# Start sequence, reciprocal rows by head pair, and key sums of pair 4 by adds, in an attention and bilinear feed-forward kernel

## The chip, the cores and the metric

The kernel runs on one core of one Trainium2 chip. Times are device microseconds of one execution; the time of a kernel is the median of its runs. The engines are named as in the profile: PE is TensorE's matmul, PEld its weight load, DVE is VectorE, ACT is ScalarE, POOL is GpSimd and SP is SyncE, which here issues most transfers. ACTq and SPq in a profile are what ScalarE and SyncE issue to their transfer queues.

## The reference

Batch 8, 12 heads, 448 tokens, head dimension 64, all in float32. Attention with normalised queries and keys is followed by a feed-forward block with two factors that are multiplied.

```
def rmsnorm(x, g):
    rms = np.sqrt(np.mean(x * x, axis=-1, keepdims=True) + 1e-06)
    return x / rms * g
q_n, k_n = (rmsnorm(q, g_q), rmsnorm(k, g_k))
scores = 1.0 / np.sqrt(q.shape[-1]) * np.matmul(q_n, k_n.transpose(0, 1, 3, 2))
scores = scores - np.max(scores, axis=-1, keepdims=True)
attn = np.exp(scores)
attn = attn / (np.sum(attn, axis=-1, keepdims=True) + 1e-09)
attn_out = np.matmul(attn, v)                  # (8, 12, 448, 64)
x = attn_out.transpose(0, 2, 1, 3).reshape(3584, 768)
out = (x @ w_a) * (x @ w_b) @ w_out            # w_a, w_b: 768 x 1536; w_out: 1536 x 768
```

## The kernel before, in words

**Attention.** The work is cut into 24 steps called pairs (`p`, three for each of the 8 batches). One step takes four heads as two head pairs `w`, each with two heads `e`. Queries and keys are loaded with half of the heads on partitions 0 to 63 and half on 64 to 127 (`loads`). For every step ScalarE squares q and k (L461, and L473 for the first q), DVE adds the squares up (L463, L485) and scales them (L496, L487), GpSimd raises them to the power -1/2 (L498, L489), and DVE multiplies q by the result (L502, L479 for the first step). TensorE transposes k and q (L537; L561 for the first step, whose q is taken in two parts), and ScalarE copies the transposes to `qkT`, q with the gains (L542, L544, L566, L568).

A step then has seven blocks `j` of keys. `scores` (L585) makes the scores of a block with keys on the partitions, in four products on four quarters of the array, and ScalarE's exponential (L591) turns them into `ET` with the keys' factor as its scale. `values` (L607) adds the block times v into `o`. A group of four products in quarters appears in the trace as 8 matmul records, since each float32 matmul is recorded twice there. Transposes are recorded once.

**Sums over the keys.** The denominators come in one of two ways. For steps below `WIDE` (5 here) `sums_over_keys` multiplies every block by ones on TensorE (L643, seven groups of four products). For the steps from `WIDE` on, `add_up` (L621) first adds the seven blocks on DVE and GpSimd in turn (`ADD_UP`: DVE for j = 1, 3, 5, 6, GpSimd for 2 and 4), and a single group of ones-products takes the sum over the partitions.

**Inversion.** `invert` has ScalarE copy the two sums into `rec` (L656). SP moves one row of each head to 56 partitions (`few`, L663), DVE takes the reciprocal of those 112 x 16 numbers (L689), and SP brings them back. For steps below `SPREAD` (6) they go back into two rows of `rec` (L672), and TensorE spreads the rows over the partitions with ones (`spread`, L679); later steps go by a tensor in memory (L668, L685). DVE multiplies the values by the result (L732).

**Feed-forward.** Two batches form a group `beta`. Its products use recombined factors, so that fewer block products are needed. The weights come as raw words (w_a, w_b and w_out; DMA at L358 and L361 from ScalarE's queue), are rounded in steps (ScalarE L247, DVE L248, L249, L251, L253, L254, L256), combined (L371) and written out to be streamed in again. There are 18 such factors; factors 0 to 11 belong to w_a and w_b, 12 to 17 to w_out. `seq` and `GATES` say in which order and after which block of scores each one starts. The long products are L1288, L865, L989 and L1186.

**What sets the order.** `Plan.op` records every operation with its engine, its costs in a planner and what it reads and writes. `Plan.run` issues the operations in an order that is stored in the text `ORDER`: a list of places, one for each operation. So each engine's sequence is fixed when the kernel is built, and an operation waits, with everything behind it on its engine, until what it reads is there. `op("SP", ...)` is a transfer that SyncE issues.

**The start.** SP issues its half of q, two rows of gains, its half of k, then v; ScalarE issues its halves of q and k, then a first half of a w_out factor. ScalarE's function table is loaded with the first square. TensorE meanwhile multiplies the identity by itself (`warm`, L408: `WARM` blocks of four at first, and `TAIL` blocks after each of the first transposes).

A second path, `general`, stands behind a test on the gains and isn't taken with these inputs.

## Time and profile before

| what | value |
|---|---|
| three runs, median (lowest to highest) | 1489.83 us (1488.78 to 1490.21) |
| the profiled execution | 1492.87 us |
| its span, first to last instruction | 1491.1 us |
| PE busy, share of the span | 1469.9 us, 99% |
| DVE / ACT / POOL busy | 985.9 / 438.7 / 333.2 us |
| mean granted clock of TensorE | 0.994 |

The busy table counts the time in which an engine executes; register, branch and semaphore instructions and the issuing of transfers are left out. Ends of matmuls are modelled, so successive starts tell the pace better than the durations. In a line of the timeline the first number is the start, the second the duration of the merged instructions, and the bracket gives the engine's idle time before it and what ended it. The chain follows the work back from the last instruction, at each step to what released it. In windows the first number in a row is the stretch, the second its length; then come each engine's busy time, the granted clock, the share of the transfer engines, and GB/s.

### The profile page before, as it was taken

The page shows a single profiled execution, that of the slowest core. Times are in us where ns is not written, and L with a number is a line of the kernel's source. Part 1 is how long each engine was busy: PE and PEld are TensorE (multiplying, and loading weights), DVE is VectorE, ACT ScalarE, POOL GpSimd, SP SyncE. Part 2 cuts the span into 40 slices and gives each one's busy share as a digit, 9 for nine tenths or more (in the row PEclk, how much of TensorE's full clock was granted, in tenths as well). Part 3 has the DMA queues.
Part 4 walks back from the last instruction along what each step waited for, and adds up shares of the span by engine and source line. Part 5 has one row for each costly group of instructions (what it writes and reads, how often), then busy time and mean ns, then how long its engine had stood idle before and what let it go on. Part 6 is the DMA issues. An engine that isn't in the chain of part 4 may idle for free.

```text
span 1491.1 us, 21095 instructions
## 1 busy us (share of the span) xinstructions
PE 1469.9 (99%) x7918; PEld 964.2 (65%) x7918; DVE 985.9 (66%) x1571; ACT 438.7 (29%) x792; POOL 333.2 (22%) x173
## 2 busy tenths in 40 slices
PE   8999999999999999999999999999999999999998
PEld 5433444555444555555544445799998899999898
DVE  5886679888765333334667776367677666776786
ACT  5776762121454000001157771011111001111100
POOL 3325551022233000111255651011110001111000
PEclk9999999999999999999999999999999999999999
DMA  9796445555363545446556654555565765555464
GB/s 252 226 256 186 110 113 177 179 200 179 113 167 92 155 147 183 136 160 190 162 142 165 143 138 134 172 157 151 166 175 169 250 180 161 153 154 157 165 211 127
DMA packets 188186, 247.99 MB, mean 166 GB/s; under 512 B 61868, under 2 KB 160684, under 8 KB 181420
## 3 DMA queue, kind: packets, MB, share of 16 engines
q1 hardware_dynamic: 158956, 192.61, 45.3%
q10 hardware_dynamic: 29120, 53.94, 10.6%
q8 instruction: 65, 1.06, 0.3%
q14 instruction: 45, 0.37, 0.1%
HBM read 188.35 MB, written 57.93 MB: 165 GB/s over the span
## 4 chain that ended last, share of the span: by engine, by line
PE 89%; DMA 5%; DVE 3%; issue 1%; ACT 1%; SPq 1%; POOL 0%; ACTq 0%; DVEq 0%; POOLq 0%
PE pq L1288 24%; PE dg L865 17%; PE po L989 16%; PE sc L585 7%; PE o L607 7%; PE da L865 6%; PE g L1186 2%; PE a L1186 2%; PE pt L537 2%; PE su L643 2%; DMA k_sb<-in_k_dram 2%; PE b L1186 1%; PE d L1186 1%; PE e L1186 1%; PE inv L679 1%
## 5 line engine op out<-in xcount | busy, mean ns | idle before, releaser
L1288 PE MATMUL pq<-x,st 128*128 128x448 f32 x1008 | 383.0, 540 | 0.9 <-DVE U L1318 0.9
L1288 PEld LDWEIGHTS pq<-x,st 128*128 128x128 f32 x1008 | 190.3, 190 | 187.8 <-issue 176.6
L591 ACT ACTIVATE ET<-sc,ms 128x448 f32<-128x448 f32 x336 | 191.1, 636 | 67.5 <-PE sc L585 49.5
L498 POOL TENSOR_TENSOR ms<-ms,expo 128x14 f32<-128x14 f32 x47 | 149.2, 3175 | 149.2 <-DVE ms L496 148.2
L865 PE MATMUL dg<-dT,st 128*128 128x224 f32 x672 | 167.2, 354 | 0.5 <-DVE dt L905 0.3
L989 PE MATMUL po<-st,hT 128*128 128x384 f32 x492 | 164.2, 488 | 0.4 <-DMA st<-kept_o 0.4
L865 PE MATMUL dg<-x,st 128*128 128x224 f32 x672 | 162.6, 354 | 0.5 <-DVE dF L912 0.5
L585 PE MATMUL sc<-qkT 64*64 64x448 f32 x1344 | 153.0, 545 | 2.0 <-ACT ET L591 1.7
L607 PE MATMUL o<-ET,v_sb 64*64 64x448 f32 x1344 | 148.9, 542 | 0.0
L893 POOL TENSOR_TENSOR hT<-dF 128x448 f32<-128x448 f32 x42 | 50.3, 1210 | 421.3 <-DVE dF L888 408.6
L989 PEld LDWEIGHTS po<-st,hT 128*128 128x128 f32 x492 | 92.3, 190 | 64.4 <-issue 3.8
L865 PEld LDWEIGHTS dg<-dT,st 128*128 128x128 f32 x672 | 126.5, 190 | 2.6 <-DVE dt L905 0.8
L865 PEld LDWEIGHTS dg<-x,st 128*128 128x128 f32 x672 | 126.2, 190 | 2.8 <-DVE dF L912 1.8
L865 PE MATMUL da<-x,st 128*128 128x224 f32 x504 | 117.3, 353 | 0.0
L621 POOL TENSOR_TENSOR sum<-sum,ET 128x896 f32<-128x896 f32 x38 | 86.9, 2286 | 106.2 <-ACT ET L591 51.7
L585 PEld LDWEIGHTS sc<-qkT 64*64 64x64 f32 x1344 | 47.2, 133 | 84.0 <-issue 44.6
L607 PEld LDWEIGHTS o<-ET,v_sb 64*64 64x64 f32 x1344 | 51.3, 134 | 74.3 <-issue 67.1
L878 ACT COPY dt<-da 128x224 f32<-128x224 f32 x84 | 28.9, 346 | 233.9 <-PE da L865 162.5
L865 PEld LDWEIGHTS da<-x,st 128*128 128x128 f32 x504 | 94.9, 190 | 0.5
L888 DVE TENSOR_TENSOR dF<-dF 128x896 f32<-128x896 f32 x84 | 92.5, 1106 | 2.2
L989 PE MATMUL po<-st,fin 128*128 128x384 f32 x252 | 86.6, 491 | 0.0
L621 DVE TENSOR_TENSOR sum<-sum,ET 128x896 f32<-128x896 f32 x57 | 62.8, 1101 | 30.0 <-POOL sum L621 18.8
(150 smaller groups left out, 1684.3 us busy)
## 6 DMA issues: line engine op xcount, KB each, us to landing
st<-kept_o SPq DMA_DIRECT2D x28, 1152.0 KB
st<-kept_s SPq DMA_DIRECT2D x84, 320.0 KB
kept<-st ACTq DMA_DIRECT2D x12, 1344.0 KB
st<-kept SPq DMA_DIRECT2D x12, 1344.0 KB
st<-kept SPq DMA_DIRECT2D x84, 192.0 KB
ti<-kept_t SPq DMA_DIRECT2D x48, 288.0 KB
kept_s<-ds SPq DMA_DIRECT2D x30, 448.0 KB
v_sb<-in_v_dram SPq DMA_DIRECT2D x48, 224.0 KB
```

The costliest lines, as they stand in the source:

```text
L498: lambda: nc.gpsimd.tensor_tensor(msf(), msf(), expo[:, 0:2 * NT * (b - a)], ALU.pow), [], names)
L537: nc.tensor.transpose(t[:, j * P:(j + 1) * P], x[:, j].rearrange("p h d -> p (h d)"), ident)
L585: nc.tensor.matmul(t[low_high[w], e, 0:S], lhsT=qkTs[p][low_high[e], 1, j * P + w * D:j * P + (w + 1) * D], rhs=qkTs[p][low_high[e], 0, w ...
L591: nc.scalar.activation(E[:, e], scs[p, j][:, e, 0:S], AF.Exp, scale=rs[p][:, 1, 2 * j + e:2 * j + e + 1])
L607: nc.tensor.matmul(os_[p][low_high[e], w, 0:S], lhsT=xs["v", p][low_high[w], e, j * D:(j + 1) * D], rhs=ETs[p, j][low_high[w], e], start=( ...
L621: two[e].tensor_tensor(sums[p], sums[p] if j > 1 else ETs[p, 0], ETs[p, j], ALU.add)
L865: nc.tensor.matmul(to(), lhsT=W(w), rhs=t(), start=not more and k == 0, stop=k == len(terms) - 1, skip_group_check=True)
L888: take("DVE", 1.09, lambda: V.tensor_tensor(F[to], F[to], F[other], ALU.add), allF(other), allF(to), lock=True)
L893: lambda: two[e].tensor_tensor(C(i, n), F[g][:, 0:S], F[g][:, S:2 * S], ALU.mult), allF(g),
L989: nc.tensor.matmul(held["po"][:, 0:HALF], lhsT=a[0]()[:, c], rhs=sts[beta, 12 + place_of[f]][:, c], start=(c == 0), stop=(c == MH - 1))
L1186: nc.tensor.matmul(held[bank], lhsT=x()[:, c], rhs=y(c), start=(start and c == 0), stop=(stop and c == MI - 1), skip_group_check=True)
L1288: nc.tensor.matmul(banks[bank][:, 0:S], lhsT=sts[at][:, f, c * P:(c + 1) * P], rhs=quads[x][:, c], start=(start and c == 0), stop=(stop an ...
```

## The change

It has four parts, and a new `ORDER`.

1. The start: a name `table` is written by the dummy exponential (L409), and the first weight loads and the first squares read it, so they stand behind it on ScalarE. In the new order ScalarE issues its halves of q and k, loads the table and runs the exponential, and issues the first weight load; the squares of q and k follow, then the second weight load. SP issues q, k, the two gain rows and v. The first warm-up has four blocks instead of three, and two follow the transposes of k instead of one.
2. The reciprocals: for steps below `SPREAD` ScalarE's copy interleaves the two head pairs in runs of 8 words, the transfers back write one row for each head pair (row 0 and row 64) instead of one for each head, and the spread takes its rows by head pair.
3. `WIDE` is 4, so pair 4 takes its key sums by adds.
4. `seq` puts factor 14 behind factors 0 and 1.

`ORDER` is a different text, so the operations outside these parts stand at other places on every engine too. By instructions, PE has 28 ones-products fewer from the seven groups of pair 4 (L643) and 4 more after its adds, and 8 warm products more; DVE has 4 adds more and POOL 2.

```diff
...
@@ -281,8 +281,8 @@
         HC, NT = HP // 2, S // D
         NC = B * HC
         STS, XS = 2, 9
-        WARM, SPLIT = 3, ((0, 4), (4, NT))
-        TAIL = {("k", None): 1, ("q", 0): 1, ("q", 1): 2}
+        WARM, SPLIT = 4, ((0, 4), (4, NT))
+        TAIL = {("k", None): 2, ("q", 0): 1, ("q", 1): 2}
         TWICE = {NB - 2: (1, 2, 3, 4, 5, 6), NB - 1: (1, 2, 3, 4, 5, 6)}
         MAKE = 1
         ONCE = NB - 2
@@ -291,7 +291,7 @@
         LOADS = "ACT"
         KEEPS = "ACT"
         APART = 24
-        WIDE, SPREAD = 5, 6
+        WIDE, SPREAD = 4, 6
         ADD_UP = [None, 'DVE', 'POOL', 'DVE', 'POOL', 'DVE', 'DVE']
 
         queue = {"ACT": nc.scalar, "SP": nc.sync}
@@ -360,7 +360,7 @@
                         at = part * HM + m * P
                         queue[LOADS].dma_start(to.rearrange("p (k n) -> p k n", k=KA),
                                             src[:, 2 * at:2 * (at + P)].rearrange("(k p) n -> p k n", p=P))
-                op(LOADS, 0.4, key - 0.75, load, after, [f"{row}/{part}"], kb=690 if last else 860)
+                op(LOADS, 0.4, key - 0.75, load, after + ["table"], [f"{row}/{part}"], kb=690 if last else 860)
             rounding(key, NW, lambda: (words().rearrange("p (n w) -> p n w", w=2), sts[n][:, 0:4].rearrange("p a b -> p (a b)")),
                      [f"{row}/{part}" for part in range(2)], f"{st}/0")
             homes = [0, 0, 0, 0, 4, 5, 6]
@@ -406,7 +406,7 @@
 
             for x in range(4):
                 nc.tensor.matmul(warms[0][:, 0, 0:P], lhsT=ident, rhs=ident, start=True, stop=True)
-        op("ACT", 1.7, -9, lambda: nc.scalar.activation(gain, nc.const_aps.tensor(0.0, [P, 1], FP32), AF.Exp), [], ["gain"])
+        op("ACT", 1.75, -9, lambda: nc.scalar.activation(gain, nc.const_aps.tensor(0.0, [P, 1], FP32), AF.Exp), [], ["gain", "table"])
         op(None, 0.0, -9, open_warm, [], ["warm"], new=[tile_of("warm", "o", 1)])
         xs, rs, qns, qkTs, pts, scs, ETs, sums, sus, os_, quads, hTs = ({} for _ in range(12))
         low_high = [slice(0, D), slice(D, P)]
@@ -481,7 +481,7 @@
                         xs["q", 0][:, :, j0 * D:j1 * D].rearrange("p h (j d) -> p h j d", d=D),
                         rs[0][:, 0, a:c].rearrange("p (h j) -> p h j ()", h=2).to_broadcast([P, 2, j1 - j0, D]), ALU.mult)
                 msf, share = (lambda: rs[0][:, 0, a:c]), (j1 - j0) / NT
-                op("ACT", 0.1 + 0.85 * share, -9, square, loaded(0, "q"), [f"{sq}/{n}"], new=[sq] if n == 0 else [])
+                op("ACT", 0.1 + 0.85 * share, -9, square, loaded(0, "q") + ["table"], [f"{sq}/{n}"], new=[sq] if n == 0 else [])
                 op("DVE", 0.14 + 0.96 * share, -9, lambda: nc.vector.tensor_reduce(msf(), xs["sq", "q", 0][:, a:c], AX, ALU.add),
                    [f"{sq}/{n}"], [mine])
                 op("DVE", 0.2, -9, lambda: nc.vector.tensor_scalar(msf(), msf(), 1.0 / D, 1e-6, ALU.mult, ALU.add), [], [mine])
@@ -653,30 +653,34 @@
             def move(w):
                 if w == 0:
                     fews["rec"] = wk.tile([P, 2, S], FP32, tag="rec", name="rec")
-                nc.scalar.copy(fews["rec"][:, w], sus[p][w])
+                if p < SPREAD:
+                    nc.scalar.copy(fews["rec"].rearrange("p a b -> p (a b)").rearrange("p (q w i) -> p w q i", w=2, i=S // FEW)[:, w],
+                                   sus[p][w].rearrange("p (q i) -> p q i", i=S // FEW))
+                else:
+                    nc.scalar.copy(fews["rec"][:, w], sus[p][w])
                 if w == 1:
                     sus[p] = fews["rec"]
 
             def spread_out():
                 fews[0] = wk.tile([2 * FEW, 2 * S // FEW], FP32, tag="few", name="few", bufs=2)
                 for e in range(2):
-                    nc.sync.dma_start(fews[0][e * FEW:(e + 1) * FEW],
-                                      sus[p][e * D:e * D + 1].rearrange("o w s -> o (w s)").rearrange("o (p i) -> o p i", p=FEW))
+                    row, to = sus[p][e * D:e * D + 1], fews[0][e * FEW:(e + 1) * FEW]
+                    nc.sync.dma_start(to, row.rearrange("o w s -> o (w s)").rearrange("o (p i) -> o p i", p=FEW))
 
             def leave():
                 fews[1] = dram.tile([2, 2 * S], FP32, name=f"inv{p}")
                 nc.sync.dma_start(fews[1].rearrange("e (p i) -> (e p) i", p=FEW), fews[0])
 
             def rows():
-                for e in range(2):
-                    nc.sync.dma_start(sus[p][e * D:e * D + 1].rearrange("o w s -> o (w s)").rearrange("o (p i) -> o p i", p=FEW),
-                                      fews[0][e * FEW:(e + 1) * FEW])
+                for w in range(2):
+                    nc.sync.dma_start(sus[p][w * D:w * D + 1].rearrange("o e s -> o (e s)").rearrange("o (p i) -> o p i", p=2 * FEW),
+                                      fews[0].rearrange("p (w i) -> p w i", w=2)[:, w])
 
             def spread():
                 t = ps_s.tile([P, 2, 512], FP32, tag="sc", name="inv")
                 for w in range(2):
                     for e in range(2):
-                        nc.tensor.matmul(t[low_high[e], w, 0:S], lhsT=ones[e * D:e * D + 1, :], rhs=sus[p][e * D:e * D + 1, w],
+                        nc.tensor.matmul(t[low_high[e], w, 0:S], lhsT=ones[w * D:w * D + 1, :], rhs=sus[p][w * D:w * D + 1, e],
                                          start=True, stop=True)
                 sus[p] = t[:, :, 0:S]
 
@@ -688,7 +692,7 @@
             op("SP", 1.65, p - 0.0, spread_out, [t], [few], new=[few], kb=8, dmas=2)
             op("DVE", 0.3, p - 0.0, lambda: nc.vector.reciprocal(fews[0], fews[0]), [], [few])
             if p < SPREAD:
-                op("SP", 1.3, p, rows, [few], [t], kb=8, dmas=2)
+                op("SP", 1.65, p, rows, [few], [t], kb=8, dmas=2)
                 inv = tile_of(f"inv{p}", "sc", 2)
                 op("PE", 0.76, p, spread, [t], [inv], new=[inv], mode="quad")
                 return
@@ -1375,7 +1379,7 @@
 
 
         GATES = [0, 2, 4, 4, 5, 5, 7, 7, 8, 8, 10, 10, 16, 18, 21, 21, 27, 32]
-        seq = [15, 13, 16, 12, 14, 0, 1, 2, 3, 4, 5, 6, 7, 8, 9, 10, 11, 17]
+        seq = [15, 13, 16, 12, 0, 1, 14, 2, 3, 4, 5, 6, 7, 8, 9, 10, 11, 17]
         def weights(at, after):
             for x, n in enumerate(seq):
                 if at == GATES[x]:
@@ -1396,7 +1400,7 @@
                 op("DVE", 0.4, 20.0, judge_gains, ["grow"], [])
                 spread_gains()
                 for x in range(WARM):
-                    op("PE", (2.5, 1.7, 1.7)[x] if x < 3 else 0.9, 1e6, warm, ["warm"], ["warm"], mode="full")
+                    op("PE", (2.1, 1.8, 1.4)[x] if x < 3 else 0.9, 1e6, warm, ["warm"], ["warm"], mode="full")
             if p < NC:
                 normalize(p)
                 transposes(p)
```

## The prediction

> **What bounds the kernel now.** I read the page's table of engines and its shares of the chain that ended last, then TensorE's waits, then the start in order of time, then windows.
>
> ```profile
> PE 1469.9 (99%) x7918; PEld 964.2 (65%) x7918; DVE 985.9 (66%) x1571; ACT 438.7 (29%) x792; POOL 333.2 (22%) x173
> PE 89%; DMA 5%; DVE 3%; issue 1%; ACT 1%; SPq 1%; POOL 0%; ACTq 0%; DVEq 0%; POOLq 0%
> ```
>
> ```profile
> PE pt L561 <- DMA k_sb<-in_k_dram: 4.5, 1, 4.5
> PE inv L679 <- DMA rec<-few: 1.8, 1, 1.8
> ```
>
> TensorE is busy for 99% of the span and carries 89% of the chain. All its recorded waits come to 14 us; asked from 130 us on alone, they come to 3.3 us. So a microsecond of TensorE work removed anywhere is nearly a microsecond off the end, and the other things worth having are the start and the few waits before 130 us. The start and the worst later place, in order of time (start, duration, instruction, and in brackets the idle time before it):
>
> ```profile
> 1.36 4.89 PE L408 MATMUL warm<-ident 128*128 128x128 f32 x24 [1.36 <-POOL ident masks.py:199]
> 2.79 0.64 SPq L432 DMA_DIRECT2D k_sb<-in_k_dram  x1
> 5.30 1.28 ACT L473 ACT_TABLE_LOAD   x1 [5.30 <-DMA q_sb<-in_q_dram]
> 10.75 1.72 PE L561 MATMUL pt<-ident,k_sb 128*128 128x128 f32 x7 [4.50 <-DMA k_sb<-in_k_dram]
> 18.78 1.74 PE L585 MATMUL sc<-qkT 64*64 64x448 f32 x16
> ...
> 124.45 4.26 PE L679 MATMUL inv<-rec,ones 1*64 1x448 f32 x8 [1.77 <-DMA rec<-few]
> 128.64 1.77 PE L585 MATMUL sc<-qkT 64*64 64x448 f32 x8
> ```
>
> The first score product begins at 18.8 us; what stands before it on TensorE is warming and transposes. The second k half is issued on SP only at 2.79, behind q and two gain rows, and lands at 10.62. At 124 us a reciprocal arrives late, and the spread that waits for it takes 4.26 us. In the windows (busy time of TensorE, its weight loads, DVE, ScalarE and GpSimd, then the granted clock) both places show half the clock, and the stretch before the second a full DVE:
>
> ```profile
> 9.00:15.00 6.00, 4.25 (x18) 3.94 (x19) 2.23 (x4) 2.01 (x4) 4.03 (x3) 0.50 1.05 299
> ...
> 125.00:131.00 6.00, 6.00 (x24) 1.60 (x26) 2.25 (x4) 1.49 (x3) 1.14 (x1) 0.50 0.20 57
> ...
> 95.00:100.00 5.00, 5.00 (x56) 1.92 (x57) 5.00 (x6) 2.47 (x5) 0.13 (x1) 1.00 1.14 231
> ```
>
> **The change, part by part.** *Key sums of pair 4.* Seven groups of ones-products become one (WIDE 5 to 4). A group is 8 matmul records. These lines of the chain price it, and the spread too:
>
> ```profile
> 67.31 1.68 PE pt L537 x14
> 68.98 0.91 PE su L643 x8
> ...
> 75.98 1.50 PE su L643 x16
> 77.48 1.65 PE inv L679 x8
> ```
>
> 16 records take 1.50, so a group is 0.75 and six are **-4.5 us** of TensorE. In their place come four adds on DVE at 1.10 (L621) and two on GpSimd at 2.29: 4.4 and 4.6 us. They lie beside TensorE: pairs 5 to 23 add this way already, and TensorE waits only 3.3 us after 130 us. Pair 4 comes earlier, where DVE is full (5.00 of 5 us from 95 to 100). The order of the changed kernel pays for them there: one w_out factor (14) is rounded later, behind factors 0 and 1, and a factor is 8.2 us of rounding (L248 to L256) and four combinations at 0.55, 10.4 us. Added up along DVE's order, the work before the fourth reciprocal is 94.3 us before and 87.1 after. If that cover were gone, pair 4's later sums would hold its reciprocal, and then its spread.
>
> *Reciprocals spread by head pair.* Each of six spreads (pairs 0 to 5) is 8 records. Before, they use two quarters of the array (row of head e to columns of head e), and 1.65 us is close to twice 0.75. Now row w goes to columns e, the four-quarter pattern of the key sums, which does the same 8 records with the same 448 columns in 0.75. Only the depth, 1 row instead of 64, differs, and the depth-1 form runs at about the pace of two quarters already. The gain is between 0 and 0.9 each; I take 0.9, by the key-sum row: six are **-5.4 us**. ScalarE's two copies of sums to a row now write runs of 8 words; I keep their 0.54 us. The two transfers from columns back to rows have 112 pieces of 32 bytes each instead of 56 of 64. The row is the transfer that landed 7.82 us after its issue at 116.49. If all of that were cost per piece, the new one would take some 7 us more; if it is queueing behind k and weights (they fill the transfer engines there, 1.0 to 1.6 in the one-microsecond windows), nothing. The Trainium skill, "DMA: Bandwidth & Descriptors", under Specifications, speaks against it: under 512 bytes a transfer loses line rate. Both sizes are under that, and only 7 KB move. By the rule the time goes toward double, by the queueing reading it stays; I take +0.5 us, nearer the second. It is hidden: between a pair's last key sum and its spread the new order has 12 to 18 us of other TensorE work (before 11 to 22). Without that cover each microsecond late is a microsecond of TensorE, six times.
>
> *The start.* SP now issues q, k, gain rows, v; ScalarE issues q and k, loads its function table and runs the dummy exponential, and only then issues weights. The k issue moves from 2.79 to about 1.55. v still follows the gain rows, so SP's queue gets no longer. The first weight transfer moves from 2.19 to about 3.75 (k at 1.52, 0.64 for it, 1.28 table, 0.19 exponential), and the second stands behind the square of k. So q and k, 0.92 MB, go first; the windows of half a microsecond show 0.95 MB moved by 6.5 us. k's 256-byte pieces are slow, so I put its landing at 7.3 (6.4 to 9). From there: square 0.95, reduction 1.09, scaling 0.17, two multiplications 0.68 and 0.55, with small gaps: about 11.0. q's own chain no longer holds the table load of 1.28 (at 5.30), and its powers on GpSimd (2.95 for both) end near 9.8, inside k's. TensorE then owes three transposes, 0.36, and the last eight warm matmuls, 1.9 (16.90 to 18.85 in the trace); ScalarE has k's copy of 0.91, two weight issues of 0.35, two more copies of 0.69 and 0.58 ahead of the first score. Both give about 14.6, within 13 and 17. That is **-4.25 us**. The two new groups of warming (8 more matmuls, 1.95 at full clock) lie before the transposes of q, in waiting time.
>
> Here the clock matters. After the warm block ended at 6.25, the granted clock fell at about 8.9, 2.6 us later. The Trainium skill, "TensorE: Matmul & The Clock Gate", Part 1 (the HAM clock gate), says that it halves after an idle window of about 3.4 us. By the rule a gap until 9 is harmless, by the row one of over 2.6 us is not. The new warm block has 32 records instead of 24, the eight more at 0.12 (16 in 1.95), and ends near 7.3, so with k at 7.3 to 9 the gap is under 1.7 and both say full clock. At 124 us, though, the clock fell after a gap of 1.77 in a thinly filled stretch, where the rule expects none; if that holds at the start too, about 2 us of the 4.25 are lost. The rule leaves -4.25, the row -2.3 at worst; I keep -4.25.
>
> *The new order.* Every engine's order is redrawn, though outside the parts above the instructions are the same. I count 88 changes between whole-array and quarter products, against 82; the first group after one takes 0.91 instead of 0.75, so **+1.0 us**. The waits of 45 to 131 us I leave as they are, between 6 us less (the place at 124 gone) and 6 more.
>
> Sum: -4.5 - 5.4 - 4.25 + 1.0 = **-13.2 us**. The profiled execution took 1492.87 (span 1491.1 and 1.8 around it); that gives 1479.7. It lies 3.0 above the median of the runs, 1489.83, so on their scale the forecast is **1476.6 us**.
>
> **Rivals.** *The late reciprocal goes as well* (1471). The wait of 1.8 and the half clock (2.6 on the spread, 0.8 each on scores and values) make 6.0, of which 5.5 are still there to win. For it: DVE has 7.2 us less ahead of that reciprocal. Against: TensorE reaches that spread with 6.0 us less work too (105.5 to 99.5 along its order, 1.9 of new warming included) and starts 4.25 earlier, as does DVE; the race stays about even.
>
> *DVE or ScalarE sets the pace up to 130 us* (1482.6). Then what TensorE saves there, 4.5 and four spreads of 0.9, 8.1 us, turns partly into waits; with three quarters lost, 6 us. For it: DVE's full windows, and ScalarE's exponentials, which TensorE waited for (1.7 and 1.4). Against: TensorE still has 89% of the chain, and DVE's load there falls.
>
> *The start doesn't move* (1480.9): k is held by its own small pieces, not by the place of its issue. Against: it landed only when nearly all that was issued with it had moved.
>
> *Slower.* The 32-byte pieces land late at the spreads. One episode as at 124 costs 6 us (wait and half clock). Two of them cost 12 and cancel the gain; from three on, 18 us against 13.2, the kernel is slower: 1494.6. It decides where the transfer takes over 3 us longer, since a pair's chain of copies, transfers and reciprocal takes some 13 us of the 12 to 18. Against: two of the six spreads show a recorded wait for that transfer at most.
>
> **How the numbers follow.** Forecast 0.55 (own range 1473 to 1480), late reciprocal gone 0.17, pace set elsewhere 0.19, start unmoved 0.04, slower 0.05. From 1470 to 1484.5 leaves out the slower case and the tails of the second and third, less than 0.2. Three microseconds, 0.2%, are about what these runs can tell from no change; below 1486.8 lie 0.92, within 0.03, above 0.05.
>
> **What would show it.** First score near 14.6 us and no half clock before it; the key sums of pair 4 in one group, and spreads of 0.75 each; TensorE's busy time shorter by about 10; waits before 131 us like before. Wrong would make it: spreads that still take 1.6, a clock at 0.50 after 7 us or in several places up to 130, ScalarE waiting at L247 for weights ahead of the first exponentials, or new waits of TensorE for DVE in the stretch of pairs 10 and 11, where DVE now has 4.4 us of adds and the late factor.

## The result, and the profile after

Five runs of the changed kernel took 1481.82 to 1484.92 us, median 1483.68. Beside it the kernel before took 1488.78 to 1492.59, median 1490.21. The ratio is 0.9951, interval 0.9936 to 0.9965: the medians differ by 6.5 us, and the interval allows 5.2 to 9.5. The forecast was 1476.6 and had counted on 13.2. So the time lies inside the range of 1470 to 1484.5, at its upper edge, and half of the gain is missing.

The profiled execution took 1483.82 us with a span of 1482.0. Against the 1491.1 of before that is 9.1 us less, because the execution profiled before stood 3 us above its own median and this one stands at its own.

The page of the changed kernel, busy time and shares of the chain:

```profile
PE 1459.8 (98%) x7886; PEld 960.0 (65%) x7886; DVE 987.5 (67%) x1575; ACT 437.9 (30%) x792; POOL 323.0 (22%) x175
PE 84%; DVE 2%; DMA 1%; issue 0%; ACT 0%; SPq 0%; DVEq 0%
```

TensorE's busy time is 10.1 us shorter, near the "about 10" of the forecast, and the work that was to go is gone. The match is in part chance: 2.6 of the 10.1 us are the spread at 124 us, which took 4.26 at half clock before and would have taken 1.65. Of the groups of instructions, those of the key sums and of the spread:

```profile
L643 PE MATMUL su<-ET,ones 64*64 64x448 f32 x224 | 24.8, 536 | 0.0
L643 PE MATMUL su<-sum,ones 64*64 64x448 f32 x160 | 19.3, 550 | 0.0
L683 PE MATMUL inv<-rec,ones 1*64 1x448 f32 x48 | 6.0, 559 | 1.1 <-DMA rec<-few 1.1
```

Before, 280 records of the first kind stood there, and the spread (L679, 48 records, too) was busy for 12.9 us. But a spread is not as short as forecast. After, the second one and what follows it:

```profile
75.66 0.98 PE L683 MATMUL inv<-rec,ones 1*64 1x448 f32 x8
76.57 1.73 PE L607 MATMUL o<-ET,v_sb 64*64 64x448 f32 x16
```

It takes 0.91 to the next start, as do four of the other five; the forecast had 0.75. Before it took 1.65, so a spread saves 0.74 and six save 4.4 us, not 5.4. Most of what is missing has to be looked for in waits and in the clock. TensorE's waits after:

```profile
PE pt L561 <- DMA k_sb<-in_k_dram: 4.2, 1, 4.2
PE sc L585 <- ACT ET L591: 3.4, 6, 1.2
PE pq L1292 <- DVE t L1333: 2.4, 1, 2.4
PE sc L585 <- ACT qkT L544: 1.9, 1, 1.9
```

The first is the wait for k that the change was to shorten, nearly as long as before (4.5). The third is new. The start in order of time:

```profile
1.36 5.22 PE L408 MATMUL warm<-ident 128*128 128x128 f32 x32 [1.36 <-POOL ident masks.py:199]
...
1.57 0.83 SPq L432 DMA_DIRECT2D k_sb<-in_k_dram  x1
2.19 1.28 ACT L409 ACT_TABLE_LOAD   x1 [2.19 <-issue]
2.27 0.63 ACTq L358 DMA_DIRECT2D hraw<-in_moe_w_out_dram  x1
...
3.37 1.72 SPq L423 DMA_DIRECT2D v_sb<-in_v_dram  x2
...
10.81 1.46 PE L561 MATMUL pt<-ident,k_sb 128*128 128x128 f32 x7 [4.23 <-DMA k_sb<-in_k_dram]
...
19.02 1.74 PE L585 MATMUL sc<-qkT 64*64 64x448 f32 x16
```

SP issues k at 1.57 instead of 2.79, as the change says. But k is there at 10.8, as before (10.75), and the first score starts at 19.0 instead of 18.8. The line at 2.27 is where the reasoning failed: the first weight transfer isn't held back by the table load. The trace of before already showed that ScalarE's queue goes on during that load, which began at 5.30 there. Its next weight transfer in it:

```profile
5.37 0.33 ACTq L358 DMA_DIRECT2D hraw<-in_moe_w_out_dram  x1
```

To see where the other microseconds went, I divide both executions at the same pieces of work: the first score, the first long product (`pq`, L1288 before, L1292 after) and the first long product of the second group. Of before and of after:

```profile
136.62 2.42 PE L1288 MATMUL pq<-x,st 128*128 128x448 f32 x6
537.53 7.68 PE L1288 MATMUL pq<-x,st 128*128 128x448 f32 x20
```

```profile
125.51 2.42 PE L1292 MATMUL pq<-x,st 128*128 128x448 f32 x6
529.72 5.80 PE L1292 MATMUL pq<-x,st 128*128 128x448 f32 x15
```

| stretch | before | after | difference | forecast of the steps that lie in it |
|---|---|---|---|---|
| to the first score | 18.8 | 19.0 | +0.2 | -4.25 |
| first score to first long product | 117.8 | 106.5 | -11.3 | -8.1 (six groups of key sums, four spreads) |
| to the second group's first long product | 400.9 | 404.2 | +3.3 | -1.8 (two spreads) |
| from there to the end | 953.6 | 952.3 | -1.3 | 0 |

The +1.0 for the new order belongs to the second and third rows. In twelve other profiled executions the last row is 951.5 to 953.0, so its 1.3 is not the change: the profiled execution of before took longer there than the others, two of which keep the old order.

The second row gained more than forecast, and the place at 124 us is gone: the clock stays at 1.00 there, and the fourth spread starts at 116.83 with no wait. Before, the half clock lasted 6.83 us at that place, which is 3.4 us of TensorE's time. The third row lost instead of gaining. Its loss shows at 220 us, in windows (stretch, length, busy time of PE, PEld, DVE, ACT, POOL, then clock, share of the transfer engines, GB/s):

```profile
220.00:225.00 5.00, 2.63 (x7) 1.37 (x6) 4.96 (x5) 1.97 (x3) 2.86 (x2) 0.77 0.35 108
225.00:230.00 5.00, 5.00 (x22) 2.17 (x24) 4.90 (x8) 1.69 (x2) 1.31 (x2) 0.89 0.67 144
```

DVE is full, TensorE is half idle, and then the clock falls. DVE's line of time there:

```profile
218.17 1.08 DVE L621 TENSOR_TENSOR sum<-ET 128x896 f32<-128x896 f32 x1
219.17 3.04 DVE L736 TENSOR_TENSOR x<-x,rec 128x448 f32<-128x448 f32 x2
222.14 0.61 DVE L1333 TENSOR_TENSOR t<-U,pq 128x448 f32<-128x448 f32 x1
```

The addition `t` that TensorE waits for stands behind two divisions of pair 8 (L736, the values times the reciprocals), which take 3.04 us together instead of 1.15, as two of them took at 167.7.

### The profile page after: what moved, and what is told of

It is laid out like the page before. It is cut to its first block, busy times and chain, and to the rows that moved or that the text cites. A ratio compares the mean times of both kernels' runs of the same rounds, so it can differ in the third digit from the quotient of the medians.

```text
span 1482.0 us, 21059 instructions
## 1 busy us (share of the span) xinstructions
PE 1459.8 (98%) x7886; PEld 960.0 (65%) x7886; DVE 987.5 (67%) x1575; ACT 437.9 (30%) x792; POOL 323.0 (22%) x175
## 4 chain that ended last, share of the span: by engine, by line
PE 84%; DVE 2%; DMA 1%; issue 0%; ACT 0%; SPq 0%; DVEq 0%
PE pq L1292 24%; PE dg L869 17%; PE po L993 16%; PE da L869 6%; PE o L607 5%; PE sc L585 5%; PE a L1190 2%; PE g L1190 2%; PE pt L537 1%; PE b L1190 1%; PE e L1190 1%; PE d L1190 1%; PE su L643 1%; DMA ti<-kept_t 1%; DMA kept_o<-st 0%; DVE x L736 0%
## 5 line engine op out<-in xcount | busy, mean ns | idle before, releaser
L1292 PE MATMUL pq<-x,st 128*128 128x448 f32 x1008 | 384.8, 542 | 2.5 <-DVE t L1333 2.4
L1292 PEld LDWEIGHTS pq<-x,st 128*128 128x128 f32 x1008 | 190.9, 191 | 191.9 <-issue 177.2
L498 POOL TENSOR_TENSOR ms<-ms,expo 128x14 f32<-128x14 f32 x47 | 141.0, 3003 | 117.6 <-DVE ms L496 103.6
L897 POOL TENSOR_TENSOR hT<-dF 128x448 f32<-128x448 f32 x42 | 47.1, 1136 | 423.1 <-DVE dF L892 323.0
```

What stands on the lines that cost most here:

```text
L498: lambda: nc.gpsimd.tensor_tensor(msf(), msf(), expo[:, 0:2 * NT * (b - a)], ALU.pow), [], names)
L897: lambda: two[e].tensor_tensor(C(i, n), F[g][:, 0:S], F[g][:, S:2 * S], ALU.mult), allF(g),
L1292: nc.tensor.matmul(banks[bank][:, 0:S], lhsT=sts[at][:, f, c * P:(c + 1) * P], rhs=quads[x][:, c], start=(start and c == 0), stop=(stop an ...
```

## The experiments

All were timed in several rounds beside the kernel before. Single executions of one kernel differ by 5 us and more, and most of that goes with the mean clock that TensorE was granted. Sorted by it, 140 runs of before and 17 of the changed kernel, from these rounds, took on average (runs in brackets):

| mean granted clock | 0.992 | 0.993 | 0.994 | 0.995 | 0.996 | 0.997 | 0.998 |
|---|---|---|---|---|---|---|---|
| before, us | 1492.3 (10) | 1490.4 (12) | 1489.3 (37) | 1488.6 (35) | 1487.3 (24) | 1485.3 (20) | 1483.1 (2) |
| changed, us | | | | | 1484.3 (4) | 1483.6 (7) | 1481.2 (6) |

At the same clock the change is worth 1.7 to 3.0 us. About half of its gain goes with the clock, whose mean over these runs rises from 0.9949 to 0.9971: half-clock episodes have become rarer. (A thousandth of 1484 us is 1.5 us, which is about the slope of the table.) So an effect is read from medians and ratios where it can be, and a profile is asked for places and for the stretches of the table above. Line numbers shift by a few where an edit adds lines.

### The spread alone, in the old order

```diff
-                nc.scalar.copy(fews["rec"][:, w], sus[p][w])
+                if p < SPREAD:
+                    nc.scalar.copy(fews["rec"].rearrange("p a b -> p (a b)").rearrange("p (q w i) -> p w q i", w=2, i=S // FEW)[:, w], ...)
...
-                        nc.tensor.matmul(t[low_high[e], w, 0:S], lhsT=ones[e * D:e * D + 1, :], rhs=sus[p][e * D:e * D + 1, w],
+                        nc.tensor.matmul(t[low_high[e], w, 0:S], lhsT=ones[w * D:w * D + 1, :], rhs=sus[p][w * D:w * D + 1, e],
```

(the transfers that belong to it are left out here)

> The kernel before with the spread by head pair alone, its order untouched. If TensorE's time is what counts: each spread takes 0.75 us to the next start instead of 1.65, six of them 5.4 us, and about 2 more of the one at half clock, so 5 to 7.5 us less than before. If the 32-byte pieces land late: TensorE waits at the spreads for the transfer and the gain is under 3 us or a loss.

Measured: 1484.75 us, ratio 0.9973 (0.9964 to 0.9982), about 4.0 us faster than before. By the stretches of its profile, first score to first long product takes 114.2 (before 117.8) and the next one 399.2 (before 400.9): 3.6 and 1.7 us less. By the starts of the matmuls a spread takes 0.91 here too, so four and two of them account for 3.0 and 1.5. The wait and the half clock near 125 us stay:

```profile
PE inv L683 <- DMA rec<-few: 2.2, 1, 2.2
...
120.00:130.00 10.00, 7.78 (x60) 2.53 (x56) 6.69 (x10) 4.72 (x9) 3.99 (x3) 0.85 0.61 211
```

So the spread pays nearly its price: 0.74 each, 4.4 for six, and the median agrees with 4.0 (2.7 to 5.4). It stays under the 5 to 7.5 that were expected. The 32-byte pieces add no wait beside the one that was there. It also says that the episode near 125 us is not cured by the shorter spread.

### The key sums of pair 4 alone, in the old order

```diff
+                if p == WIDE - 1:
+                    if j:
+                        two[ADD_UP[j]].tensor_tensor(sums[p], sums[p] if j > 1 else ETs[p, 0], ETs[p, j], ALU.add)
+                    if last:   # one group of ones-products on sums[p]
```

The first of the seven groups goes, each of the other six becomes an addition at its own place, and the last addition is followed by the single group.

> The kernel before with pair 4's seven key-sum groups replaced by six adds at their places in the order and one group, nothing else moved. If TensorE's time is what counts: 4.5 us less. If DVE sets the pace between 60 and 130 us: its 4.4 us of adds stand in a full stretch without the later rounding of factor 14, and the gain is under 2 us or a loss, with new waits of TensorE there.

Measured: 1491.64 us, ratio 1.0026 (1.0017 to 1.0035), 3.9 us slower than before. TensorE's waits and the windows from 110 us:

```profile
PE sc L585 <- ACT ET L591: 6.2, 5, 3.5
PE su L644 <- DVE sum L639: 4.9, 1, 4.9
...
110.00:120.00 10.00, 5.33 (x47) 1.89 (x46) 9.86 (x13) 5.70 (x9) 7.61 (x3) 0.90 1.14 261
120.00:130.00 10.00, 6.26 (x38) 2.12 (x40) 5.78 (x5) 3.28 (x6) 4.14 (x2) 0.59 0.36 123
```

DVE is busy for 9.86 of 10 us while TensorE stands for half of the time. In the old order the 4.5 us of TensorE are lost and more. That fits the prediction, which named the late rounding of factor 14 as the cover; the late rounding without the rest of the new order was not run, so it is not shown that this alone makes the part pay.

### k ahead of weights and v; k in long pieces

The first kernel moves two places in the order that is stored: the first half of a weight load behind the square of k, and v of pair 0 behind the second load of q.

```diff
+    MOVED = ((11, 45), (9, 195))
...
+        order = [rest.pop(places[k] + 256 * places[n + k]) for k in range(n)]
+        for x, y in self.MOVED:
+            order.remove(x)
+            order.insert(order.index(y) + 1, x)
```

> The changed kernel with the first weight load behind the square of k and v of pair 0 behind the second load of q, so that only q, k and the gain rows are under way until k has landed. If k is held by its company on the transfer engines: it lands 2 to 4 us earlier than 10.7, the first score begins at 15 to 17 instead of 19.0, and the kernel is 2 to 4 us faster than the changed one (about 9 to 10 less than before). If k is held by its own 256-byte pieces: it lands at 10 to 10.7 as before and the time stays with the changed kernel (about 6.5 less than before).

The second loads k of pair 0 in runs of 1792 bytes, and DVE copies it into place.

```diff
-                        xs[nm, p][low_high[w]], pair.rearrange("h (p j) d -> p j h d" if nm == "k" else "h (p j) d -> p h (j d)", j=NT))
+                        (first_k() if nm == "k" else xs[nm, p])[low_high[w]], pair.rearrange("h (p j) d -> p h (j d)", j=NT))
```

> The changed kernel with k of pair 0 loaded in runs of 1792 bytes like q, and put in the order of the transposes by one copy on DVE. If its own 256-byte pieces hold k: it lands at 6 to 8 us instead of 10.7, the first score begins at 14.5 to 16.5, and the kernel is 2.5 to 4.5 us faster than the changed one (about 9 to 11 less than before). If its company holds it: it lands near 10.7 still and the time stays or is 1 us longer for the copy.

Measured: 1484.9 us for the first, ratio 0.9968 (0.9956 to 0.998), and 1484.8 for the second, 0.9969 (0.9955 to 0.9982): neither is better than the changed kernel. But their starts differ. In long pieces k still comes at 10.3, so its small pieces don't hold it. With weights and v out of the way:

```profile
7.99 0.95 PE L565 MATMUL pt<-ident,k_sb 128*128 128x128 f32 x7 [0.17 <-DMA k_sb<-in_k_dram]
...
14.56 1.73 PE L589 MATMUL sc<-qkT 64*64 64x448 f32 x16
...
23.54 3.21 PE L611 MATMUL o<-ET,v_sb 64*64 64x448 f32 x14 [3.41 <-DMA v_sb<-in_v_dram]
```

The first score stands at 14.56, where the prediction had put it (14.6), with full clock. So the chain of steps from k's landing to the first score was about right (6.6 us where the forecast had 7.3), and the landing in the changed kernel was not. Here v comes 3.4 us late, and the gain is given back at once.

### The weight transfer alone moved, the divisions moved, and both

Three kernels beside a repeat of the changed kernel, which is the measure for them. 11 is the first half of the first weight load and 45 the square of k; 1113 and 1114 are the divisions of pair 8, 683 and 685 the two additions `t`.

```diff
+    MOVED = ((11, 45),)                                   weights_later
+    MOVED = ((1113, 685), (1114, 1113))                   divide_later
+    MOVED = ((11, 45), (1113, 685), (1114, 1113))         both
```

> The changed kernel as it is, beside the three that follow, so that their differences of a few microseconds can be read against it on the same chip. Expected: 6 to 7.5 us under the kernel before (ratio 0.995 to 0.996), and in its profile the wait of pq for DVE's t of 2.4 us with half clock near 220 us, if that belongs to the order of the work; if it was an accident of one execution, it is gone or elsewhere.

> The changed kernel with one step moved: ScalarE issues the first weight transfer behind the square of k instead of at 2.27 us; v of pair 0 keeps its place (in k_first it was moved as well, and came late). Theory (the first weight transfer shares the transfer engines with k and holds it up, v does little): k lands at 8 to 8.5, first score at 14.6 to 15.2, no half clock at the start, v on time, and the whole 3 to 4.5 us faster than the changed kernel. Rival (v holds k as much as the weights do): k lands at 9.3 or later, half clock as before, first score over 16.5, and 0 to 2.5 us faster.

> The changed kernel with DVE's two divisions of pair 8 behind the two multiplications t that TensorE waits for near 220 us. Theory (the new order put the divisions, one of which takes 2.4 us beside a GpSimd addition, in front of t, and the wait of 2.4 us brings the clock down as well): wait and half clock at 220 us are gone, pq takes its 4.5 us for 12 instead of 6.4, and the kernel is 3 to 4 us faster than the changed one. Rival (the time is given back at the next wait, or the place was an accident of one execution): within 1 us of the changed kernel.

> Both moves at once. If each removes a loss of its own, they add: 6 to 8 us faster than the changed kernel, near 1476.5 where the kernel before takes 1490. If TensorE's start only shifts waits to the stretch from 45 to 130 us, as DVE and ScalarE set the pace there, it is no better than divide_later alone.

| kernel | median us | ratio to before (interval) | against the changed kernel, difference of means |
|---|---|---|---|
| changed kernel again | 1483.03 | 0.9965 (0.9951 to 0.9978) | |
| weights_later | 1479.45 | 0.9947 (0.9930 to 0.9964) | -2.9 (-4.7 to -1.0) |
| divide_later | 1480.36 | 0.9952 (0.9934 to 0.9971) | -2.3 (-4.6 to 0.0) |
| both | 1481.14 | 0.9955 (0.9940 to 0.9971) | -1.7 (-3.1 to -0.2) |

The last column takes the means of 12, 6, 6 and 6 runs, with their scatter. The changed kernel itself came out 5.2 us under the kernel before (3.3 to 7.3), a little less than the 6 to 7.5 expected, and the wait of 2.4 for `t` stood in its profile again.

*weights_later* has the lowest median of all and is faster than both kernels. Its start:

```profile
8.31 0.95 PE L565 MATMUL pt<-ident,k_sb 128*128 128x128 f32 x7 [0.17 <-DMA k_sb<-in_k_dram]
...
14.89 1.73 PE L589 MATMUL sc<-qkT 64*64 64x448 f32 x16
```

One transfer, moved by 6 us, brings k forward by 2.5 and the first score by 4.1, and v is 0.4 late at most. The theory holds: the weights hold k, and v hardly does (7.99 with v moved as well). With the early weights k landed at 8.8 to 11.7 in six executions, with the late ones at 8.0 to 8.3 in four.

*divide_later* removes the wait of 2.4, and another takes its place one product later:

```profile
PE pq L1296 <- DVE t L1353: 1.3, 1, 1.3
...
PE pq L1296 <- DVE hT L1340: 0.3, 1, 0.3
```

From the first long product to the second group it takes 402.3 us. The changed kernel took 404.2 in the first execution, with the half clock after 220, and 402.6 in the second, which had the same wait of 2.4 but kept a clock of 1.00. Other kernels with that wait agree: 404.1 to 404.6 with the half clock (weights_later, k_first, q5_first), 402.8 and 402.9 without (six_more, k_long). So the order of the divisions is worth about 0.4 us, and 1.9 where the clock falls. Most of the wait was given back, as the rival said. The rest of this kernel's lead lies before the first long product and may be scatter; the expected 3 to 4 us aren't shown.

*both* is not better than either: the two don't add. Its runs agree within 0.7 us, 1480.8 to 1481.43. Its start is that of weights_later, but between 90 and 100 us TensorE is busy for 6.5 of 10 us where weights_later has 8.8. ScalarE's square of q waits 2.4 us there for a transfer that was issued 11 us earlier (in weights_later it waits 1.4). From the first score to the first long product this execution takes 3.3 us longer than that of weights_later, most of the start's gain.

### The old spread in the new order, and six groups put back

```diff
-                        nc.tensor.matmul(t[low_high[e], w, 0:S], lhsT=ones[w * D:w * D + 1, :], rhs=sus[p][w * D:w * D + 1, e],
+                        nc.tensor.matmul(t[low_high[e], w, 0:S], lhsT=ones[e * D:e * D + 1, :], rhs=sus[p][e * D:e * D + 1, w],
```

(with the copies and transfers that belong to it)

> The changed kernel with the old spread (two quarters, 64-byte pieces, ScalarE's plain copies) in the new order. Theory (TensorE is the bound and six spreads of 1.65 instead of 0.75 stand in its way): 5 us slower than the changed kernel, near 0.999 to 1.000 of the kernel before. Rival (waits of the stretch up to 130 us take up what a shorter spread leaves, so only the two or three later spreads count): 2 to 3 us slower than the changed kernel.

```diff
-                for w in range(2):
+                for w in (0, 1, 0, 1) if p == WIDE and j else (0, 1):
                     for e in range(2):
                         nc.tensor.matmul(t[low_high[w], e, 0:S], lhsT=qkTs[p][low_high[e], 1, ...
```

> The changed kernel with the score products of pair 4 for key blocks 1 to 6 made twice into the same place: six more groups of 0.75, the six that pair 4's key sums gave up, and nothing more for DVE. If TensorE is the bound in that stretch, 4.5 us slower than the changed kernel. If DVE, ScalarE or the transfers set the pace between 90 and 130 us, TensorE has room there and it is 0 to 2 us slower.

Measured: 1485.73 us, ratio 0.9984 (0.9976 to 0.9992), and 1486.5 us, 0.9987 (0.9978 to 0.9996). Set against the 0.9965 of the repeat of the changed kernel, the old spread costs 2.8 us, plus or minus 2.3, and the six groups cost 3.3, plus or minus 2.4 (the intervals added in squares). Set against the 0.9951 of its first comparison, they cost 4.9 and 5.4. By the starts of the matmuls the spreads are worth 4.4 and the groups 4.5. So the two values of the changed kernel differ by as much as is asked for, and these runs don't decide whether part of the price was lost. The stretches can't decide: from first score to first long product the old spread takes 107.7 and six more groups take 109.0, where the changed kernel has 106.5 and 106.7 in two executions, and kernels that are alike there (weights_later, divide_later, both) 106.7, 104.2 and 110.0. What the windows show is that TensorE has idle time there. For the changed kernel and with six more groups:

```profile
90.00:130.00 40.00, 35.95 (x338) 14.38 (x334) 30.59 (x39) 30.05 (x48) 22.51 (x9) 1.00 0.72 186
```

```profile
90.00:130.00 40.00, 39.08 (x374) 16.04 (x378) 28.77 (x38) 29.63 (x49) 23.66 (x9) 1.00 0.65 165
```

TensorE is busy for 36.0 of the 40 us in the one and for 39.1 in the other; in the second execution of the changed kernel it was 37.5. So 2.5 to 4 us are idle in which extra groups could hide. How much of the saved work was saved next to waits stays open.

### Factor 14 rounded in part

DVE's steps on factor 14 take the first eighth of the columns; the rest of that factor stays unrounded.

```diff
+            some = round_steps(lambda: tuple(x[:, 0:NW // 8] for x in get()))
+            for i, (e, n, emit, r, wr) in enumerate(round_steps(get)):
+                if e == "DVE" and key == 3.7:
+                    emit = some[i][2]
```

> The changed kernel, in which DVE rounds only the first eighth of factor 14, the one that the new order rounds late (about 8.2 us of DVE become 1.5 near 190 to 200 us; the rest of that factor stays unrounded). Theory (DVE sets the pace from 190 to 250 us, since that factor stands there now): the wait of pq for t near 220 us is gone, and it is 3 to 5 us faster than the changed kernel. Rival (the wait of 2.4 comes from the two divisions beside GpSimd's addition alone): the wait stays, and it is within 1.5 us of the changed kernel.

Measured: 1483.43 us, ratio 0.9966 (0.9955 to 0.9976): no gain over the changed kernel. DVE is busy 5.6 instead of 9.8 of 10 us between 200 and 210, and the wait stays:

```profile
PE pq L1295 <- DVE t L1336: 2.4, 1, 2.4
...
208.43 1.61 ACT L247 ACTIVATE st<-lraw 128x1536 f32<-128x1536 f32 x1 [4.04 <-DMA kept_o<-st]
...
210.07 0.96 DVE L248 TENSOR_SCALAR st<-st 128x1536 f32<-128x1536 f32 x1 [1.56 <-ACT st L247]
```

My theory that DVE's load from 190 to 210 makes the wait near 220 is wrong. DVE has spare time, and then it waits for ScalarE's first step of the next factor, which the profile puts down to the landing of a store, `kept_o<-st`. In the changed kernel that step waits 2.88 us for the same store. From it on the chain is closed: five steps of rounding, an addition, two divisions, `t`. So, by these traces, the wait near 220 follows from a factor that starts when a store has landed, with the divisions in the way; no run moved that store.

### Half of a weight load out of the way of q

weights_later showed q of pair 5 landing 10 us after its issue, behind a store and two weight halves. 137 is the second of these halves, 568 the square of that q.

```diff
-    MOVED = ((11, 45),)
+    MOVED = ((11, 45), (137, 568))
```

> weights_later with one more step moved: the second half of the weight load near 83 us is issued behind the square of pair 5's q, instead of ahead of it. Theory (a store and two weight halves fill the transfer engines from 79 to 97 us and hold q of pair 5, which lands 10 us after its issue, so ScalarE and then TensorE wait): q lands 2 to 3 us earlier, TensorE's busy time in 90 to 100 us goes from 8.8 to over 9.5, and it is 1 to 2 us faster than weights_later. Rival (k or v, which land later still, or the weights themselves set the time): no gain, or up to 2 us slower with ScalarE waiting for the weight half near 95 us.

Measured: 1485.85 us, ratio 0.9986 (0.9974 to 0.9998), some 6 us slower than weights_later. The theory fell:

```profile
91.55 0.95 ACT L465 ACTIVATE sq<-q_sb 128x896 f32<-128x896 f32 x1 [3.35 <-DMA q_sb<-in_q_dram]
...
100.47 1.58 ACT L251 ACTIVATE st<-lraw 128x1536 f32<-128x1536 f32 x1 [4.31 <-issue]
```

q comes no earlier (91.55 against 89.38 in weights_later), and ScalarE stands 4.3 us before the next factor's first step, which reads the weight half that is issued late now (the profile itself names no releaser), with TensorE waiting 3.9 us for the exponentials behind it and a clock of 0.66 from 100 to 110. What holds this q stays open; the weight half isn't it.

## Why the prediction was right, and where it failed

**The price of the saved work** was right for the key sums, which lost six groups, and a little high for the spread. It was taken at the 0.75 of a key-sum group, but a spread takes 0.91 to the next start, what the prediction itself has for the first group after a change of mode. So -5.4 should have been -4.4, and done alone the spread gave 4.0 by the median. The forecast for the 32-byte pieces, "+0.5 us" and hidden, stands: one wait for them after, 1.1 us.

**The start, -4.25,** is the step that failed, and in one sentence of it: "The first weight transfer moves from 2.19 to about 3.75", behind the table load and the dummy exponential. It is issued at 2.27, while the table is being loaded. Two things were taken together there: the engine, which is busy with the table for 1.28 us, and its queue, which issues transfers meanwhile. So k shared the transfer engines with the weights again. The Trainium skill, "DMA: Bandwidth & Descriptors", under "Issuing engines are not separate DMA queues", says that transfers of all issuing engines run on the same 16 engines and interleave. The runs agree: k on SP's and ScalarE's queues came at 10.8 beside the weights on ScalarE's, and at 8.3 without them. My rival *the start doesn't move* had 0.04 and the wrong reason, the small pieces; k_long rules that reason out.

The rest of that step is confirmed by weights_later: 14.89 for a forecast of 14.6. In the changed kernel the start is also a lottery. Over six executions with its start the first score came at 19.0, 19.9, 19.1, 17.3, 17.4 and 15.4. The first three had the half clock (k waited for 4.2 to 4.7 us), and in the last k landed at 8.8. Four executions with the weights moved gave 14.6 to 14.9.

**The place at 124 us** went, which was the rival *the late reciprocal goes as well*, given 0.17. Against it I had held that "the race stays about even". The runs with one part alone show that neither part cures the place in the old order (a reciprocal 2.2 us late and a clock of 0.85 with the spread, a sum 4.9 us late and 0.59 with the key sums), so most likely the new order does: in none of the runs of the new order does TensorE wait for a reciprocal of pairs 1 to 5. Both parts together in the old order were not run. It is worth about 3 us beyond the forecast in the second row of the table, in that execution of before, as much as the half clock had cost; others of before had a mean clock of up to 0.998, so not every one can have had it in full.

**DVE or ScalarE sets the pace up to 130 us**, given 0.19, isn't settled: against one value of the changed kernel six_more and spread_back put the worth of the saved work below its length, against the other not, and TensorE has 2.5 to 4 us of idle time from 90 to 130. "TensorE waits only 3.3 us after 130 us", the cover that I had named, said nothing of this stretch. There a wait for `qkT` is new, 1.9 us at 94 us in the first execution and 1.1 in the second.

**The new order, +1.0,** was mis-sized. I had priced its changes of mode, not its waits. From the first long product to the second group, two spreads should have brought the 400.9 to 399.1, and spread_alone, with the old order, shows 399.2. The new order shows 402.6 and 404.2: 3.5 to 5.1 us more, of which 2.4 are the wait for `t` and 1.6 the half clock that follows in some executions. The prediction's last sentence had named the place ("new waits of TensorE for DVE in the stretch of pairs 10 and 11"), but no term of the sum stood for it. Its cause is not DVE's load from 190 to 210 us, as light_14 shows, and moving the divisions only shifts it. What would have to be moved to win these microseconds was not found.

**The sum.** Row by row, the profiled executions miss the forecast by 4.45 at the start and by 5.1 in the third row, and beat it by 3.2 in the second and by 1.3 in the last; with the 1.0 that was put down for the new order that leaves -9.1 of -13.2. The other 3.0 were lost in the step from the profiled execution to the median: "It lies 3.0 above the median of the runs, 1489.83", and the forecast was set lower by as much. That took the 3.0 for an offset that stays. The runs sorted by clock explain only a part of it: executions of before at 0.994 average 1489.3, so this one took 3.6 us longer than its clock tells, and 1.3 of them lie in the last row. It was scatter of one execution, and the execution profiled after had none.

About half of the gain that was measured goes with the clock. Of the 8.9 us of saved work (4.5 and 4.4), 1.7 to 3.0 are left when the clock is equal: the start brought nothing to speak of, and the new order took a part in waits, 2.4 for `t` and up to 1.9 for `qkT`. Where the rest went was not found. That the time still lies inside the range, by 0.8 us, is partly luck: the 3.2 us of the second row, which no term of the sum stood for, made up for part of what the start and the new order lost.

## What to carry to other kernels

A transfer that an engine issues is not behind that engine's running instruction, but it is behind an instruction that still waits for its data: to hold it back, put it behind such a wait, as weights_later does with the square of k. A saved microsecond of the bounding engine is worth a microsecond only in stretches where nothing else waits (sums_alone saved TensorE 4.5 us and lost 3.9); price the two sides of a stretch by putting the work back in. A new order has to be priced by its waits and by the clock, not by its instructions alone; and a profiled execution that stands above its median holds something that the median does not, so find out what before its difference is carried over.

## What the runs showed of the hardware

*A queue beside its engine.* ScalarE's queue issued a transfer at 2.27, 0.08 us after the table load of 1.28 us had begun; in the other six executions with the early weights it was 0.07 to 0.08. What held the transfer in weights_later was not the square of k as it ran, but its wait for k:

```profile
8.29 0.95 ACT L465 ACTIVATE sq<-k_sb 128x896 f32<-128x896 f32 x1 [1.66 <-DMA k_sb<-in_k_dram]
8.31 0.85 ACTq L362 DMA_DIRECT2D hraw<-in_moe_w_out_dram  x2
```

*The clock.* In every trace of this case the granted clock changes only on a grid of 3.41 us, and the half clock between them lasts one, two or three steps: 3.41, 6.83 or 10.24 us (the last one of a trace is cut off by its end). The Trainium skill, "TensorE: Matmul & The Clock Gate", Part 1, says that activity is judged over a window of about 3.4 us that runs freely; the grid agrees. So the length of a gap alone doesn't decide. In the wait near 220 us the clock fell in four executions, after gaps of 2.25 to 2.41 us, and stayed full in five, after 2.23 to 2.43. What differs is how the gap lies on the grid. The step with the gap, and the next one, in the two executions of the changed kernel:

```profile
219.32:222.74 3.42, 1.11 (x8) 0.69 (x6) 3.42 (x3) 1.50 (x3) 2.39 (x1) 1.00 0.71 228
222.74:226.15 3.41, 3.35 (x5) 1.71 (x6) 3.38 (x4) 0.47 (x2) 1.13 (x1) 0.50 0.02 2
```

```profile
220.10:223.51 3.41, 1.44 (x9) 0.83 (x7) 3.41 (x4) 1.11 (x2) 2.40 (x1) 1.00 0.84 278
223.51:226.92 3.41, 2.96 (x8) 1.63 (x9) 3.38 (x4) 0.86 (x2) 1.13 (x1) 1.00 0.07 17
```

After every full-clock step with TensorE busy for 1.2 us or less, 28 in the traces (14 of them at the kernel's end), the next step had half the clock; the least busy step after which it stayed full is the one with 1.44. Five falls don't fit, after steps busy for 1.4 to 3.25 us, before at 124 us among them (1.64). All five lie among the quarter products of the attention, and what counts there stays open.

*DVE beside GpSimd.* A division with both operands in SBUF (`x<-x,rec`) takes 0.61. Of two in a row the second took 2.50 in each case in which GpSimd's addition (`sum<-sum,ET`) began beside the first: at 187.5 and 219.2 after, at 221.5 before, and each time it was done 0.5 us after the addition. Beside the same addition at 120.1 two divisions by `inv`, which lies in PSUM, took 0.62 each. GpSimd's small powers (L498) did not slow a division (0.62 at 167.7 after).
